# Two attention blocks on one core: output projection of the last chunks taken head by head, and loads issued in order of deadline

## The chip, the cores and the metric

The kernel runs on one core of one Trainium2 chip. The metric is the device time of one execution in microseconds (us). A profile comes from one execution, whose span is about 1.7 us shorter than its device time.

## The reference

Two independent problems, A and B, of the same shape are computed and their results laid side by side. B = 16 batches, 144 queries each, model width 448, 16 heads of width 256, and a cache of 512 keys and values per batch and head, all bf16:

```python
q = (x @ wq).reshape(B, Sq, H, Dh).transpose(0, 2, 1, 3)
scores = einsum("bhqd,bhkd->bhqk", q, k_cache) * (Dh ** -0.5)
p = softmax(scores, axis=-1)
o = einsum("bhqk,bhkd->bhqd", p, v_cache)
return o.transpose(0, 2, 1, 3).reshape(B, Sq, H * Dh) @ wo
```

The caches are nearly all of the data: 67 MB of K and 67 MB of V for each problem.

## The kernel before

The kernel is one software pipeline over 512 units (problem, batch, head). A small scheduler in Python walks through *slots*; in slot i each engine receives one step of several units at different stages. TensorE (PE) gets, in this order: Q projection of unit i+15, every eighth slot the scores of the last 32 query rows of eight units at once (**SB**), scores of the first 112 rows of unit i+5 (**SA**), transposes of the probabilities of unit i+2 (**TA**, and every fourth slot **TB**), probabilities times values of unit i (**PV**), and then some matmuls of the output projection (**OP**). K is loaded with a DMA transpose in groups of eight units (2 MB), V in groups of four (1 MB); three buffers hold each. The SyncE queue (SP) issues all loads strictly in program order, and a load whose buffer is still in use makes SP wait.

The loads were planned by slot:

```python
plan(s_min, t_load_x, 0)
plan(s_min, t_load_wq, 0, 0)                    # ... 0,1 and 0,2
plan(s_min, t_load_k, 0)                        # K group 0
# ... the fourth wq group, V groups 0 and 1
for wg in range(NWG):
    plan(s_min + 1, t_load_wo, 0, wg)           # all of wo, ahead of K group 1
# ...
for SG in range(1, NSG):
    plan(max(s_min, 8 * (SG - NK) + 7 - LS + 1, 8 * SG - 19), t_load_k, SG)   # needed in slot 8*SG-7
for G in range(2, NG):
    plan(max(s_min + 2, 4 * G - 8, 4 * (G - NV) + 3 + 1), t_load_v, G)        # needed in slot 4*G
```

The output is projected in chunks of 128 rows: 32 matmuls that add up in one PSUM bank. A chunk starts only when all heads of its batches are there:

```python
if h == H - 1:                                   # last head of a batch
    # ... for each chunk r that is now complete:
    for p in range(NPC):
        fifo.append((r, p, i + OP_DELAY))
if i >= 0:
    credit += OP_RATE                            # 2.25 matmuls a slot
if i >= NT:
    credit += 4 * OPP
while fifo and fifo[0][2] <= i and credit >= OPP:    # OPP = 2
    credit -= OPP
    # ... take one pair of matmuls; after the last pair evict the bank and store
```

## Time and profile before

| | before |
|---|---|
| time, median of the first 4 runs | 1220.0 us (1219.55 to 1220.79) |
| span of the profile | 1217.8 us |
| PE busy | 1173.1 us, 96% |
| PE waiting for K group 1 | 13.6 us |
| PE waiting for x and wq at the start | 10.5 us |
| after the last PV | 20.0 us |

From the page of before: the span, busy time of each engine with its share of the span, and the shares of the chain of waits that ended last.

```profile
span 1217.8 us, 33870 instructions
PE 1173.1 (96%) x13952; PEld 903.2 (74%) x13952; DVE 770.3 (63%) x2178; ACT 747.9 (61%) x2214; POOL 677.6 (56%) x682
PE 93%; SPq 3%; DMA 2%; DVE 1%; ACT 1%; POOL 0%; issue 0%; ACTq 0%
```

PE is both the busiest engine and the chain. What can be won without touching its work is the time in which it stands still, as far as the trace shows it as idle (e5 finds time that it doesn't show). The wait table of PE in before says where (total us, times, longest):

```profile
PE sb_ps L341 <- DMA kt_sb<-in_A_k_cache_dram: 13.6, 1, 13.6
PE qp_ps L314 <- DMA wq_sb<-in_A_wq_dram: 10.5, 1, 10.5
PE op_ps L538 <- ACT ost_sb L551: 4.4, 4, 1.3
```

SP's timeline in before (start, us of issue, what) shows why K group 1 is late:

```profile
7.83 13.56 SPq L290 DMA_TRANSPOSE kt_sb<-in_A_k_cache_dram  x1
...
22.60 1.14 SPq L299 DMA_DIRECT2D v_sb<-in_A_v_cache_dram  x2
23.79 14.16 SPq L269 DMA_DIRECT2D wo_sb<-in_A_wo_dram  x8
37.99 21.01 SPq L290 DMA_TRANSPOSE kt_sb<-in_A_k_cache_dram  x2
```

Eight wo loads, not needed before slot 17, take 14.16 us of issue ahead of a K that is needed in slot 1. PE's timeline at that place ends each line with the idle time before it and its releaser:

```profile
37.91 0.66 PE L314 MATMUL qp_ps<-xt_sb,wq_sb 128*128 128x144 bf16 x8
52.14 1.90 PE L341 MATMUL sb_ps<-kt_sb,qt_sb 128*32 128x512 bf16 x16 [13.56 <-DMA kt_sb<-in_A_k_cache_dram]
```

And the tail, again PE's timeline: the last two PV, then two chunks of 32 OP matmuls that stand alone:

```profile
1196.68 1.16 PE L503 MATMUL ot_ps<-pt_sb,v_sb 128*128 128x144 bf16 x16
1198.34 6.23 PE L538 MATMUL op_ps<-wo_sb,ring 128*128 128x448 bf16 x32 [0.50 <-ACT ring L518]
1205.27 6.23 PE L538 MATMUL op_ps<-wo_sb,ring 128*128 128x448 bf16 x32 [0.69 <-ACT ost_sb L551]
```

### The profile page before, as it was taken

To read this page: it belongs to the slowest core of one execution; us is meant where nothing else is said; L and a number is where in the kernel's file an instruction comes from. 1 tells how busy PE (TensorE), PEld (TensorE's weight loads), DVE (VectorE), ACT (ScalarE), POOL (GpSimd) and SP (SyncE) were. 2 spreads that over 40 slices of the span, in tenths; PEclk is the share of its full clock that TensorE was granted. 3 is DMA by queue.
4 is the path that set the end of the run, shared out by engine and by line. 5 is a ranking of instruction groups with operands and counts; after the bars stand their busy time and mean duration, and the time that the engine had idled before them with its cause. 6 is when DMAs were issued, how large, how long until landed. Compare 5 with 4: busy or idle time off the path is not lost.

```text
span 1217.8 us, 33870 instructions
## 1 busy us (share of the span) xinstructions
PE 1173.1 (96%) x13952; PEld 903.2 (74%) x13952; DVE 770.3 (63%) x2178; ACT 747.9 (61%) x2214; POOL 677.6 (56%) x682
## 2 busy tenths in 40 slices
PE   4499999999999999999999999999999999999997
PEld 3377777777777777777777777777777777777774
DVE  2377666666666666666666666666666666666661
ACT  1366666666666665666666665666666666666662
POOL 0356556555655655655655655655655665565562
PEclk9799999999999999999999999999999999999999
DMA  9999999999999999999999999999999999999940
GB/s 256 283 242 268 258 262 246 247 234 238 231 255 245 242 241 237 241 244 244 285 268 264 308 276 260 234 244 259 233 239 237 256 236 233 228 243 237 243 153 12
DMA packets 627033, 294.15 MB, mean 242 GB/s; under 512 B 548416, under 2 KB 556608, under 8 KB 626880
## 3 DMA queue, kind: packets, MB, share of 16 engines
q1 hardware_dynamic: 625152, 287.85, 102.9%
q0 software_dynamic: 1728, 4.13, 1.4%
q8 instruction: 111, 1.82, 0.6%
q14 instruction: 42, 0.34, 0.1%
HBM read 148.90 MB, written 4.13 MB: 126 GB/s over the span
## 4 chain that ended last, share of the span: by engine, by line
PE 93%; SPq 3%; DMA 2%; DVE 1%; ACT 1%; POOL 0%; issue 0%; ACTq 0%
PE ot_ps L503 20%; PE qp_ps L314 20%; PE sa_ps L417 19%; PE op_ps L538 18%; PE sa_ps L470 8%; PE sb_ps L341 5%; PE sb_ps L393 2%; DMA kt_sb<-in_A_k_cache_dram 1%; SPq L269 1%; SPq L290 1%; DMA v_sb<-in_B_v_cache_dram 1%; DVE stat L428 1%; SPq L261 0%; ACT pa_sb L439 0%; ACT ost_sb L551 0%
## 5 line engine op out<-in xcount | busy, mean ns | idle before, releaser
L457 POOL TENSOR_TENSOR pa_sb<-pa_sb,stat 112x512 bf16<-112x512 bf16 x512 | 532.0, 1039 | 490.9 <-DVE stat L449 490.6
L439 ACT ACTIVATE pa_sb<-sa_ps,stat 112x512 bf16<-112x512 f32 x512 | 352.0, 688 | 424.2 <-DVE stat L428 423.8
L428 DVE TENSOR_REDUCE stat<-sa_ps 112x1 f32<-112x512 f32 x512 | 353.8, 691 | 301.5 <-PE sa_ps L417 299.0
L314 PEld LDWEIGHTS qp_ps<-xt_sb,wq_sb 128*128 128x128 bf16 x4096 | 292.4, 99 | 99.7 <-issue 11.3
L314 PE MATMUL qp_ps<-xt_sb,wq_sb 128*128 128x144 bf16 x4096 | 344.6, 228 | 16.3 <-DMA wq_sb<-in_A_wq_dram 10.5
L503 PE MATMUL ot_ps<-pt_sb,v_sb 128*128 128x144 bf16 x4096 | 340.8, 226 | 0.8 <-DMA v_sb<-in_B_v_cache_dram 0.8
L417 PE MATMUL sa_ps<-kt_sb,qt_sb 128*112 128x512 bf16 x1024 | 310.1, 384 | 1.2 <-DVE pt_sb L480 0.8
L538 PE MATMUL op_ps<-wo_sb,ring 128*128 128x448 bf16 x1152 | 291.6, 352 | 4.9 <-ACT ost_sb L551 4.4
L503 PEld LDWEIGHTS ot_ps<-pt_sb,v_sb 128*128 128x128 bf16 x4096 | 268.9, 98 | 1.1 <-DMA v_sb<-in_B_v_cache_dram 0.9
L470 PEld LDWEIGHTS sa_ps<-ident,pa_sb 112*128 112x128 bf16 x2048 | 163.1, 113 | 102.7 <-ACT pa_sb L439 17.3
L518 ACT ACTIVATE ring<-ot_ps 128x288 bf16<-128x288 f32 (+8 forms) x512 | 190.0, 371 | 2.5 <-PE ot_ps L503 2.4
L480 DVE COPY pt_sb<-sa_ps 128x448 bf16<-128x448 bf16 x512 | 190.2, 371 | 1.7 <-PE sa_ps L470 1.7
L325 DVE TENSOR_SCALAR qt_sb<-qp_ps 128x288 bf16<-128x288 f32 x256 | 117.0, 457 | 116.0 <-PE qp_ps L314 116.0
L470 PE MATMUL sa_ps<-ident,pa_sb 112*128 112x112 bf16 x2048 | 186.0, 213 | 0.5 <-ACT pa_sb L439 0.5
L381 POOL TENSOR_TENSOR pb_sb<-pb_sb,stat 128x512 bf16<-128x512 bf16 x128 | 132.9, 1039 | 27.2 <-DVE stat L373 27.2
L417 PEld LDWEIGHTS sa_ps<-kt_sb,qt_sb 128*112 128x112 bf16 x1024 | 97.2, 130 | 36.6 <-issue 27.2
L329 ACT ACTIVATE qt_sb<-qp_ps 128x288 bf16<-128x288 f32 x256 | 105.9, 414 | 21.9 <-PE qp_ps L314 21.9
L538 PEld LDWEIGHTS op_ps<-wo_sb,ring 128*128 128x128 bf16 x1152 | 96.6, 98 | 29.7 <-ACT ost_sb L551 6.2
L439 ACT ACTIVATION_READ_ACCUMULATOR pa_sb<-sa_ps,stat 112x1 f32 x512 | 99.2, 194 | 0.0
L353 DVE TENSOR_REDUCE stat<-sb_ps 128x1 f32<-128x512 f32 x128 | 86.9, 679 | 4.6 <-PE sb_ps L341 4.6
L363 ACT ACTIVATE pb_sb<-sb_ps,stat 128x512 bf16<-128x512 f32 x128 | 88.4, 691 | 2.1 <-DVE stat L353 2.1
L341 PE MATMUL sb_ps<-kt_sb,qt_sb 128*32 128x512 bf16 x1024 | 68.6, 389 | 14.7 <-DMA kt_sb<-in_A_k_cache_dram 13.6
(20 smaller groups left out, 366.5 us busy)
## 6 DMA issues: line engine op xcount, KB each, us to landing
v_sb<-in_A_v_cache_dram SPq DMA_DIRECT2D x64, 1024.0 KB, 6.2
v_sb<-in_B_v_cache_dram SPq DMA_DIRECT2D x64, 1024.0 KB, 6.2
out_dram<-ost_sb POOLq DMA_DIRECT2D x36, 112.0 KB, 6.7
wo_sb<-in_A_wo_dram SPq DMA_DIRECT2D x8, 448.0 KB, 8.5
wo_sb<-in_B_wo_dram SPq DMA_DIRECT2D x8, 448.0 KB, 7.2
wq_sb<-in_A_wq_dram SPq DMA_DIRECT2D x4, 768.0 KB, 6.4
wq_sb<-in_B_wq_dram SPq DMA_DIRECT2D x4, 768.0 KB, 7.6
wq_sb<-in_A_wq_dram SPq DMA_DIRECT2D x4, 128.0 KB, 7.0
```

Source lines behind the costliest of these rows:

```text
L314: ins = t.matmul(qp_ps[:, dc * SQ:(dc + 1) * SQ], lhsT=wq_sb[:, kc, c0:c0 + 128], rhs=xt_sb[:, xsl, kc, xo:xo + SQ], start=(kc == 0), stop ...
L341: ins = t.matmul(sb_ps[jj // 4][32 * j:32 * j + 32, :], lhsT=qt_sb[:, U % NQT, dc, QA:SQ], rhs=kt_sb[:, ksl, dc, jj * SK:(jj + 1) * SK], s ...
L381: return g.tensor_tensor(pb_sb[:, psl, :], pb_sb[:, psl, :], stat[:, RINVB + sl:RINVB + sl + 1].to_broadcast([128, SK]), op=ALU.mult)
L417: ins = t.matmul(sa_ps[bank][0:QA, :], lhsT=qt_sb[:, U % NQT, dc, 0:QA], rhs=kt_sb[:, ksl, dc, ko:ko + SK], start=(dc == 0), stop=(dc == 1))
L428: return v.tensor_reduce(stat[0:QA, NEG + sl:NEG + sl + 1], sa_ps[bank][0:QA, :], axis=AX.X, op=ALU.max, negate=True)
L439: return a.activation(pa_sb[0:QA, psl, :], sa_ps[bank][0:QA, :], AF.Exp, bias=stat[0:QA, NEG + sl:NEG + sl + 1], scale=1.0, accum_out=stat ...
L457: return g.tensor_tensor(pa_sb[0:QA, psl, :], pa_sb[0:QA, psl, :], stat[0:QA, RINV + sl:RINV + sl + 1].to_broadcast([QA, SK]), op=ALU.mult)
L470: ins = t.transpose(pta_ps[bank][:, c * 128:c * 128 + QA], src[:, c, :], ident[0:QA, 0:QA])
L480: return v.tensor_copy(pt_sb[:, sl, :, 0:QA], pta_ps[bank][:, 0:512].rearrange("p (c q) -> p c q", c=4)[:, :, 0:QA])
L503: ins = t.matmul(ot_ps[ob][:, dc * SQ:(dc + 1) * SQ], lhsT=v_sb[:, vsl, j, c * DH + dc * 128:c * DH + (dc + 1) * 128], rhs=pt_sb[:, sl, c, ...
L518: ins = a.activation(ring[:, 2 * h:2 * h + 2, c0:c0 + n1], src[:, :, 0:n1], AF.Copy)
L538: ins = t.matmul(op_ps[0:m, 0:D], lhsT=ring[:, c, col0:col0 + m], rhs=wo_sb[:, c, :], start=(c == 0), stop=(c == NWO - 1))
```

## The change

Its intent: (1) the last two chunks are projected head by head during the last 16 units, one in the OP bank and one in the Q projection's bank, which is free by then; (2) every load gets a deadline (the slot of its first use), and loads are issued in the order of deadlines, so that wo no longer stands ahead of K. With it came smaller things: after an eviction of the OP bank no OP for the rest of that slot and in the next one (`op_hold`, the "two-slot hold" below); OP is taken with a credit of 1 instead of 2; more credit in the last 30 slots; the Q projection accumulates with the two halves interleaved; the first SB goes ahead of a Q; there is a third output buffer, and the chunk in the Q bank is evicted by VectorE (DVE).

Cut to its core:

```diff
-            if i >= NT:
+            if i >= u_tail0 - 14:
+                credit += 4.0
+            if i >= NT:
                 credit += 4 * OPP
-            while fifo and fifo[0][2] <= i and credit >= OPP:
-                credit -= OPP
-                r, p, _s = fifo.pop(0)
-                t_op_piece(r, p)
+            for bank in ("op", "qp"):
+                while fifo[bank] and fifo[bank][0][2] <= i and credit >= 1 and (bank == "qp" or i >= op_hold):
+                    r, cs = pop_items(bank, i, OPP)
+                    credit -= len(cs)
+                    t_op_piece(r, cs, bank)
   ... (evict and store after the last piece)
+                        if bank == "op":
+                            op_hold = i + 2
   ... (per head, in the last 16 units)
+                if u >= u_tail0:
+                    for r in tail_chunks:
+                        for dc in range(2):
+                            fifo[tail_bank[r]].append((r, 2 * h + dc, i + 1))
   ... (loads)
+        for wg in range(NWG):
+            plan(s_min, H - 4 + 2 * wg, 10 ** 6, t_load_wo, 0, wg)
+        for SG in range(NSG):
+            dl = 8 * SG - LSB
+            lo = 8 * (SG - NK) + 7 - LS + 1 if SG >= NK else s_min
+            plan(lo, dl, 12, t_load_k, SG)
+        for G in range(NG):
+            dl = 4 * G
+            lo = 4 * (G - NV) + 3 + 1 if G >= NV else s_min
+            plan(lo, dl, 8, t_load_v, G)
+        dma_plan.sort(key=lambda t: t[:2])       # by deadline
+        for dl, sq, lo, lead, fn, args in dma_plan:
+            _prev = max(_prev, lo, dl - lead)    # a running maximum: nothing overtakes
```

Interleaving the two halves of Q in one bank needs care with the start flag, which only the first matmul now carries. The Trainium skill (PSUM — Partial Sum Buffer, "The four PSUM rules") says that this flag clears the written marks of the whole 2 KiB bank, so that the second half's first matmul overwrites, too.

A V that must wait for its buffer now holds back a K with a later deadline, although that K's own lead is longer.

More of the change, by code (lines that the diff above doesn't have):

```diff
@@ L164, in bass_concat_heads__mha_block_cached__gqa_block_cached__near_ridge_kernel @@
     XB = 4 if Bn % 4 == 0 else (2 if Bn % 2 == 0 else 1)
-    NQT, NPA, NPB, NPT, NST, NSTB, NOST = 12, 5, 2, 8, 4, 2, 2
+    NQT, NPA, NPB, NPT, NST, NSTB, NOST = 12, 5, 2, 8, 4, 2, 3
     RS = 4
@@ L310, in e @@
                 ins = None
-                for dc in range(2):
-                    for kc in range(4):
+                for kc in range(4):
+                    for dc in range(2):
                         c0 = h * DH + dc * 128
                         ins = t.matmul(qp_ps[:, dc * SQ:(dc + 1) * SQ], lhsT=wq_sb[:, kc, c0:c0 + 128],
-                                       rhs=xt_sb[:, xsl, kc, xo:xo + SQ], start=(kc == 0), stop=(kc == 3))
+                                       rhs=xt_sb[:, xsl, kc, xo:xo + SQ], start=(kc == 0 and dc == 0),
+                                       stop=(kc == 3), skip_group_check=True)
                 return ins
-            S.add(PE, e, reads=[(("wq", hg), pr), ("wqz", 0), (("xt", xsl), XG)], writes=[("qp", U)],
+            S.add(PE, e, reads=[(("wq", hg), pr), ("wqz", 0), (("xt", xsl), XG)], writes=[("qp", ("q", U))],
                   banks=["qp"], name="Q%d" % U)
@@ L325, in e @@
                     return v.tensor_scalar(qt_sb[:, sl, :, :], src, 1.0 / 16.0, None, op0=ALU.mult)
-                S.add(DVE, e, reads=[("qp", U)], writes=[(("qt", sl), U)], banks=["qp"], name="eq%d" % U)
+                S.add(DVE, e, reads=[("qp", ("q", U))], writes=[(("qt", sl), U)], banks=["qp"], name="eq%d" % U)
             else:
@@ L329, in e @@
                     return a.activation(qt_sb[:, sl, :, :], src, AF.Copy, scale=1.0 / 16.0)
-                S.add(ACT, e, reads=[("qp", U)], writes=[(("qt", sl), U)], banks=["qp"], name="eq%d" % U)
+                S.add(ACT, e, reads=[("qp", ("q", U))], writes=[(("qt", sl), U)], banks=["qp"], name="eq%d" % U)
         def t_sb(SG):
@@ L521, in e @@
                 return ins
-            S.add(ACT, e, reads=[(("otp", ob), U)], writes=[(("ring", r % RS), r) for r in chunks_of_batch(pr, b)],
+            S.add(ACT, e, reads=[(("otp", ob), U)], writes=[(("ring", r % RS, h), r) for r in chunks_of_batch(pr, b)],
                   banks=["ot%d" % ob], name="eot%d" % U)
@@ L529, in chunk_rows, with t_op_piece @@
             return pr, row0, m
-        def t_op_piece(r, p):
+        def t_op_piece(r, cs, bank):
             pr, row0, m = chunk_rows(r)
             col0 = (r % RS) * 128
+            acc = op_ps if bank == "op" else qp_ps
+            key = "opp" if bank == "op" else "qp"
+            first, last = op_first[r], op_last[r]
             def e(t):
                 ins = None
-                for c in range(p * OPP, (p + 1) * OPP):
-                    ins = t.matmul(op_ps[0:m, 0:D], lhsT=ring[:, c, col0:col0 + m], rhs=wo_sb[:, c, :],
-                                   start=(c == 0), stop=(c == NWO - 1))
+                for c in cs:
+                    ins = t.matmul(acc[0:m, 0:D], lhsT=ring[:, c, col0:col0 + m], rhs=wo_sb[:, c, :],
+                                   start=(c == first), stop=(c == last))
@@ L540, in e @@
                 return ins
             nb = len([b for b in range(Bn) if r in chunks_of_batch(pr, b)])
-            assert len(S.res[("ring", r % RS)].writers) == nb * H, (r, nb, len(S.res[("ring", r % RS)].writers))
-            S.add(PE, e, reads=[(("ring", r % RS), r), (("wo", (p * OPP) // WOG), pr)], writes=[("opp", r)],
-                  banks=["op"], name="OP%d.%d" % (r, p))
-        def t_evac_op(r):
+            rd = []
+            for hh in sorted(set(c // 2 for c in cs)):
+                assert len(S.res[("ring", r % RS, hh)].writers) == nb, (r, hh, nb)
+                rd.append((("ring", r % RS, hh), r))
@@ L547, in t_evac_op, with e @@
+            S.add(PE, e, reads=rd + [(("wo", wg), pr) for wg in sorted(set(c // WOG for c in cs))],
+                  writes=[(key, ("o", r))], banks=[bank], name="OP%d.%d" % (r, cs[0]))
+        def t_evac_op(r, bank, eng):
             pr, row0, m = chunk_rows(r)
             sl = r % NOST
-            def e(a):
-                return a.activation(ost_sb[0:m, sl, :], op_ps[0:m, 0:D], AF.Copy)
-            S.add(ACT, e, reads=[("opp", r)], writes=[(("ost", sl), r)], banks=["op"], name="eop%d" % r)
+            acc = op_ps if bank == "op" else qp_ps
+            key = "opp" if bank == "op" else "qp"
+            if eng == ACT:
+                def e(a):
+                    return a.activation(ost_sb[0:m, sl, :], acc[0:m, 0:D], AF.Copy)
+            else:
+                def e(v):
+                    return v.tensor_copy(ost_sb[0:m, sl, :], acc[0:m, 0:D])
+            S.add(eng, e, reads=[(key, ("o", r))], writes=[(("ost", sl), r)], banks=[bank], name="eop%d" % r)
@@ L566, in bass_concat_heads__mha_block_cached__gqa_block_cached__near_ridge_kernel, with plan @@
         t_ident()
-        dma_plan = {}
-        def plan(slot, fn, *args):
-            dma_plan.setdefault(slot, []).append((fn, args))
+        dma_plan = []
+        def plan(lo, deadline, lead, fn, *args):
+            dma_plan.append((deadline, len(dma_plan), lo, lead, fn, args))
         s_min = -LQ - 24
-        plan(s_min, t_load_x, 0)
-        plan(s_min, t_load_wq, 0, 0)
-        if HG > 1:
-            plan(s_min, t_load_wq, 0, 1)
-        if HG > 2:
-            plan(s_min, t_load_wq, 0, 2)
@@ L579, in bass_concat_heads__mha_block_cached__gqa_block_cached__near_ridge_kernel @@
-        plan(s_min, t_load_k, 0)
-        for hg in range(3, HG):
-            plan(s_min, t_load_wq, 0, hg)
-        plan(s_min, t_load_v, 0)
-        if NG > 1:
-            plan(s_min, t_load_v, 1)
-        for wg in range(NWG):
-            plan(s_min + 1, t_load_wo, 0, wg)
-        x_last_reader = {}
         for XG in range(NXGT):
             pr, j = divmod(XG, Bn // XB)
-            u_last = pr * NU + (j + 1) * XB * H - 1
-            x_last_reader[XG] = u_last - LQ
-        for XG in range(1, NXGT):
-            pr, j = divmod(XG, Bn // XB)
@@ L594, in bass_concat_heads__mha_block_cached__gqa_block_cached__near_ridge_kernel @@
             u_first = pr * NU + j * XB * H
-            lo = x_last_reader[XG - NXG] + 1 if XG >= NXG else s_min
-            plan(max(s_min, lo, u_first - LQ - 40), t_load_x, XG)
-        for SG in range(1, NSG):
-            plan(max(s_min, 8 * (SG - NK) + 7 - LS + 1, 8 * SG - 19), t_load_k, SG)
-        for G in range(2, NG):
-            plan(max(s_min + 2, 4 * G - 8, 4 * (G - NV) + 3 + 1), t_load_v, G)
-        for pr in range(1, NP):
-            for hg in range(HG):
-                plan(pr * NU - H + 4 * hg + 3 - LQ + 1, t_load_wq, pr, hg)
@@ L605, in bass_concat_heads__mha_block_cached__gqa_block_cached__near_ridge_kernel @@
-        fifo = []
+            dl = u_first - LQ
+            if XG >= NXG:
+                pr0, j0 = divmod(XG - NXG, Bn // XB)
+                lo = pr0 * NU + (j0 + 1) * XB * H - 1 - LQ + 1
+            else:
+                lo = s_min
+            plan(lo, dl, 40, t_load_x, XG)
+        for pr in range(NP):
+            for hg in range(HG):
+                dl = pr * NU + 4 * hg - LQ
+                lo = pr * NU - H + 4 * hg + 3 - LQ + 1 if pr > 0 else s_min
+                plan(lo, dl, 10 ** 6, t_load_wq, pr, hg)
@@ new lines, in bass_concat_heads__mha_block_cached__gqa_block_cached__near_ridge_kernel @@
+        for wg in range(NWG):
[9 more added lines that the diff above has]
+        dma_plan.sort(key=lambda t: t[:2])
+        _prev = s_min
+        _tmp = []
@@ new lines, in bass_concat_heads__mha_block_cached__gqa_block_cached__near_ridge_kernel @@
+        for dl, sq, lo, lead, fn, args in dma_plan:
+            _prev = max(_prev, lo, dl - lead)
+            _tmp.append((_prev, dl, sq, fn, args))
+        dma_plan = _tmp
+        u_tail0 = NT - H
+        pr_l, b_l, _h = unit(NT - 1)
+        tail_chunks = []
+        g_end_l = pr_l * RP + (b_l + 1) * SQ
+        for r in range((pr_l * RP + b_l * SQ) // 128, (g_end_l - 1) // 128 + 1):
+            tail_chunks.append(r)
+        tail_chunks = tail_chunks[-2:]
+        tail_bank = {}
+        if tail_chunks:
+            tail_bank[tail_chunks[-1]] = "qp"
+            if len(tail_chunks) > 1:
+                tail_bank[tail_chunks[0]] = "op"
@@ L606, in bass_concat_heads__mha_block_cached__gqa_block_cached__near_ridge_kernel, with queue_chunk, pop_items @@
+        op_first, op_last = {}, {}
+        fifo = {"op": [], "qp": []}
         stores = []
         credit = 0.0
+        op_hold = -10 ** 9
         OP_RATE = float(NCH * NWO) / NU
         last_chunk_of = {pr: (pr + 1) * NCH - 1 for pr in range(NP)}
+        def queue_chunk(r, ready):
+            op_first[r], op_last[r] = 0, NWO - 1
+            for c in range(NWO):
+                fifo["op"].append((r, c, ready))
+        def pop_items(bank, i, n):
+            q = fifo[bank]
+            r = q[0][0]
+            cs = []
+            while q and len(cs) < n and q[0][0] == r and q[0][2] <= i:
+                cs.append(q.pop(0)[1])
+            return r, cs
@@ L610, in bass_concat_heads__mha_block_cached__gqa_block_cached__near_ridge_kernel @@
         i = s_min
         while True:
-            for fn, args in dma_plan.pop(i, []):
+            while dma_plan and dma_plan[0][0] <= i:
+                _sl, _dl, _sq, fn, args = dma_plan.pop(0)
                 fn(*args)
@@ L629, in bass_concat_heads__mha_block_cached__gqa_block_cached__near_ridge_kernel @@
                 t_store(stores.pop(0)[0])
+            if do_sb and sgi == 0:
+                t_sb(sgi)
             u = i + LQ
@@ L633, in bass_concat_heads__mha_block_cached__gqa_block_cached__near_ridge_kernel @@
                 t_evac_q(u)
-            if do_sb:
+            if do_sb and sgi > 0:
                 t_sb(sgi)
@@ L663, in bass_concat_heads__mha_block_cached__gqa_block_cached__near_ridge_kernel @@
                 pr, b, h = unit(u)
+                if u >= u_tail0:
+                    for r in tail_chunks:
+                        if h == 0:
+                            op_first[r], op_last[r] = 0, NWO - 1
+                        for dc in range(2):
+                            fifo[tail_bank[r]].append((r, 2 * h + dc, i + 1))
                 if h == H - 1:
@@ L668, in bass_concat_heads__mha_block_cached__gqa_block_cached__near_ridge_kernel @@
                         r_end = min((r + 1) * 128, pr * RP + Bn * SQ)
-                        if g_end >= r_end:
-                            for p in range(NPC):
-                                fifo.append((r, p, i + OP_DELAY))
+                        if g_end >= r_end and r not in tail_bank:
+                            queue_chunk(r, i + OP_DELAY)
             if i >= 0:
                 credit += OP_RATE
+            if i >= u_tail0 - 14:
+                credit += 4.0
             if i >= NT:
                 credit += 4 * OPP
-            while fifo and fifo[0][2] <= i and credit >= OPP:
-                credit -= OPP
-                r, p, _s = fifo.pop(0)
-                t_op_piece(r, p)
-                pr = r // NCH
-                if r == last_chunk_of[pr] and pr + 1 < NP and (p * OPP) % WOG == WOG - OPP:
-                    t_load_wo(pr + 1, (p * OPP) // WOG)
-                if p == NPC - 1:
-                    t_evac_op(r)
-                    stores.append((r, i + 2))
-            if not fifo:
+            for bank in ("op", "qp"):
[3 more added lines that the diff above has]
+                    t_op_piece(r, cs, bank)
+                    pr = r // NCH
+                    if r == last_chunk_of[pr] and pr + 1 < NP:
+                        for c in cs:
+                            if c % WOG == WOG - 1:
+                                t_load_wo(pr + 1, c // WOG)
+                    if cs[-1] == op_last[r]:
+                        t_evac_op(r, bank, ACT if bank == "op" else DVE)
+                        stores.append((r, i + (2 if i < NT else 0)))
+                        if bank == "op":
+                            op_hold = i + 2
+            if not fifo["op"] and not fifo["qp"]:
                 credit = min(credit, 2.0 * OPP)
             i += 1
-            if i >= NT and not fifo and not dma_plan and not stores:
+            if i >= NT and not fifo["op"] and not fifo["qp"] and not dma_plan and not stores:
                 break
```

## The prediction

> **What bounds it now.** TensorE. The page gives PE 1173.1 of 1217.8 us (96%), the chain of waits is 93% PE. PE's idle 45 us: 10.5 us at the start for x and wq (wait table); 13.6 us at 38.5-52.1 us for the second K group; half-microsecond waits for evictions during the first Q projections; 4.4 us before output projections (OP) for the eviction of op_ps; and the end. DMA is close behind: about 242 GB/s throughout, SP issuing without a pause until about 145 us.
>
> **Loads at the start.** SP's timeline shows K0's issue ending at 21.4, then wq3, V0, V1, then eight wo loads (14.2 us of issue), and only then K1, issued at 38.0, landed at 52.1. The change issues K1 right after V0 and spreads wo behind it. K1 then lands at about 39, so the stall shrinks to 0-2 us. The stall also chilled PE: the windows view shows clock 0.50 at 52-56 us, and SB took 1.90 us against 1.05. The Trainium skill (TensorE: Matmul & The Clock Gate, "The HAM clock gate") says that an idle window of about 3.4 us halves the clock; the trace agrees. Together 13.6 + 2 us.
>
> Not all of it stays. The queue is saturated: a period of one K and two V costs about 16.4 us, PE consumes one in 15.8-19.6 us, and the wo loads are only postponed. I estimate K2..K7 landing 0-3 us late each; net gain by the eighth group about 6 us (3-12).
>
> **Loads later.** Sorting by deadline with a running maximum of slots puts K behind a V that waits for its buffer: K is issued about 9 slots (20 us, sometimes 18.5) before its use, before 12. Median issue-to-landing is 15.7 us, so it usually holds, but x loads (4.2 + 1.3 us of issue) now sit directly ahead of a K, and at the change of problem x and wq0 do. Where before paid only 0.8 us (for V, near 700 us), I expect 3-8 us of K waits at 590-720 us, and 0-2 us at each other x load. Loss about 6 us.
>
> **Tail.** Before, after the last PV (1197.8), 32 + 32 OP matmuls run alone (2 x 6.24 us). The change spreads them per head over the last 16 units, in two banks. But PE is nearly full there: a slot without Q lasts 1.78 us through the loop SA, max, reciprocal, copy, with about 0.2 us free next to one OP pair. So 12.5 us move and are not removed. Removed are only PE gaps: 0.5 + 0.7 + 0.7 + about 1 us. Final eviction, store and landing (6 us) stay. Gain 2-3 us.
>
> **Other.** The two-slot hold after an op_ps eviction saves up to 3 us in the middle. Q's loop order and SB0 ahead of Q8: within 1 us.
>
> Sum: -6 + 6 - 2.5 - 3 = about -6 us: **1214 us**, range **1203 to 1226**. Chances: faster by over 2% 0.04, within 2% 0.93, slower 0.03.
>
> **What would show it.** Right: no 13.6 us wait for K1, clock near 1.0 from 30 us on; smaller PE waits for kt_sb (total 5-20 us) in the first 150 us, near 590-720 us and at x loads; last PV 6-9 us before the end instead of 20; PE busy about 1170. Wrong: K waits nowhere later (then about 1200), or in most groups (then over 1225).
>
> **What would make it wrong.** Transfers landing faster or slower than the medians in this order; OP bursts (22 in one slot) starving the DVE loop; a stall over 3.4 us cooling PE again.

## The result, and the profile after

| | before | changed |
|---|---|---|
| time, median | 1219.81 us (13 runs) | 1215.43 us (9 runs, 1213.76 to 1216.72) |
| ratio, 95% interval | | 0.9963 (0.9954 to 0.9973) |
| span of the profile | 1217.8 us | 1209.9 us |
| PE busy | 1173.1 us | 1175.1 us |
| PE waits for K | 13.6 us, 1 time | 9.1 us, 7 times |
| from the end of the last PV to the end | 20.0 us | 8.1 us |

A ratio is the mean time of one kernel's runs over the mean of the other's in the same rounds, so it is not quite the ratio of the medians quoted. The changed kernel is 0.4% faster, and this is clear of noise. The outputs are right. Its profiled execution took 1211.66 us, less than any of the nine timed ones, so the profile is used for places, and the rounds for the size of the whole.

From the page after:

```profile
span 1209.9 us, 33868 instructions
PE 1175.1 (97%) x13952; PEld 902.0 (75%) x13952; DVE 769.7 (64%) x2179; ACT 752.8 (62%) x2213; POOL 678.7 (56%) x682
PE 90%; DMA 6%; DVE 1%; SPq 1%; ACT 0%; issue 0%; POOL 0%; ACTq 0%
```

The chain now runs 6% of the span through DMA, where it was 2%. PE's wait table after:

```profile
PE qp_ps L314 <- DMA wq_sb<-in_A_wq_dram: 10.6, 1, 10.6
PE sb_ps L342 <- DMA kt_sb<-in_A_k_cache_dram: 6.3, 5, 1.8
...
PE sb_ps L342 <- DMA kt_sb<-in_B_k_cache_dram: 2.8, 2, 2.3
```

One long wait for K became seven short ones; the wait for the OP eviction is gone. SP's timeline after, at the start:

```profile
22.86 0.59 SPq L299 DMA_DIRECT2D v_sb<-in_A_v_cache_dram  x1
23.49 13.32 SPq L290 DMA_TRANSPOSE kt_sb<-in_A_k_cache_dram  x1
36.86 1.13 SPq L299 DMA_DIRECT2D v_sb<-in_A_v_cache_dram  x2
38.03 14.45 SPq L290 DMA_TRANSPOSE kt_sb<-in_A_k_cache_dram  x1
52.53 0.58 SPq L269 DMA_DIRECT2D wo_sb<-in_A_wo_dram  x1
```

K group 1 is issued at 23.49 us, not 37.99, and wo begins at 52.53. PE's timeline there:

```profile
38.84 0.66 PE L314 MATMUL qp_ps<-xt_sb,wq_sb 128*128 128x144 bf16 x8
39.54 1.05 PE L342 MATMUL sb_ps<-kt_sb,qt_sb 128*32 128x512 bf16 x16
```

SB starts at 39.54 us instead of 52.14 and takes 1.05 us instead of 1.90. The tail after (PE's timeline):

```profile
1201.20 0.66 PE L504 MATMUL ot_ps<-pt_sb,v_sb 128*128 128x144 bf16 x8
1201.70 0.54 PE L542 MATMUL op_ps<-wo_sb,ring 128*128 128x448 bf16 x2
1202.08 0.54 PE L542 MATMUL qp_ps<-wo_sb,ring 128*128 128x448 bf16 x2
1202.46 0.54 PE L542 MATMUL op_ps<-wo_sb,ring 128*128 128x448 bf16 x2
1202.84 0.54 PE L542 MATMUL qp_ps<-wo_sb,ring 128*128 128x448 bf16 x2
```

Only eight OP matmuls follow the last PV. But the last PV itself ends at 1201.86 us, *later* than before (1197.84).

**The ledger.** Both kernels run 64 SBs, one for each K group, so the start of each SB is a milestone that can be compared between traces. The table cuts the profile of each kernel at the SBs of groups 8, 31, 36 and 61 (177, 592, 683 and 1138 us in before) and gives how much each stretch is longer (+) or shorter (−) than in before. The rows below the second belong to the experiments. An *empty slot* is one in which no OP matmul is issued.

| us against before, by stretch | start to 8 | 8 to 31 | 31 to 36 | 36 to 61 | 61 to end | span |
|---|---|---|---|---|---|---|
| changed, first profile | −8.1 | +0.7 | +3.2 | −1.8 | −1.8 | −7.9 |
| changed, second profile (r_after) | −7.9 | +0.7 | +3.4 | −1.8 | −1.7 | −7.3 |
| loads only (e1) | −6.9 | +0.2 | +3.8 | −1.0 | 0.0 | −3.8 |
| all but loads (e2) | +0.4 | +0.7 | +0.3 | −1.8 | −1.7 | −2.1 |
| changed, no hold (e3) | −4.8 | +1.3 | +4.7 | −0.6 | −0.5 | +0.2 |
| changed, no added empty slots (e5) | −5.0 | −0.9 | +4.6 | −3.0 | −1.9 | −6.2 |
| changed, no wo traffic (e6) | −12.7 | +0.7 | +3.8 | −1.8 | −1.7 | −11.7 |
| changed, loads in slots of before, wo late (e4) | −7.0 | +0.7 | +0.3 | −1.3 | −1.7 | −9.0 |
| changed, K ahead again after the start (e10) | −8.2 | +0.7 | +0.3 | −1.5 | −1.7 | −10.4 |
| put together (e9) | −9.2 | −2.3 | −0.6 | −3.4 | −3.1 | −18.7 |

### The profile page after: what moved, and what is told of

It reads as the page before. It is cut to its first block, busy times and chain, and to the rows that moved or that the text cites. A ratio compares the mean times of both kernels' runs of the same rounds, so it can differ in the third digit from the quotient of the medians.

```text
span 1209.9 us, 33868 instructions
## 1 busy us (share of the span) xinstructions
PE 1175.1 (97%) x13952; PEld 902.0 (75%) x13952; DVE 769.7 (64%) x2179; ACT 752.8 (62%) x2213; POOL 678.7 (56%) x682
## 4 chain that ended last, share of the span: by engine, by line
PE 90%; DMA 6%; DVE 1%; SPq 1%; ACT 0%; issue 0%; POOL 0%; ACTq 0%
PE qp_ps L314 20%; PE ot_ps L504 19%; PE sa_ps L418 18%; PE op_ps L542 17%; PE sa_ps L471 8%; PE sb_ps L342 5%; DMA kt_sb<-in_A_k_cache_dram 4%; PE sb_ps L394 2%; DMA kt_sb<-in_B_k_cache_dram 2%; DVE stat L429 1%; DMA wq_sb<-in_A_wq_dram 1%; PE qp_ps L542 0%; SPq L280 0%; SPq L281 0%; DVE qt_sb L326 0%
## 5 line engine op out<-in xcount | busy, mean ns | idle before, releaser
L314 PE MATMUL qp_ps<-xt_sb,wq_sb 128*128 128x144 bf16 x4096 | 344.3, 228 | 16.4 <-DMA wq_sb<-in_A_wq_dram 10.6
L542 PE MATMUL op_ps<-wo_sb,ring 128*128 128x448 bf16 x1120 | 278.8, 352 | 0.0
L450 DVE RECIPROCAL stat<-stat 112x1 f32<-112x1 f32 x512 | 78.1, 152 | 0.5 <-ACT pa_sb L440 0.5
```

What stands on the lines that cost most here:

```text
L314: ins = t.matmul(qp_ps[:, dc * SQ:(dc + 1) * SQ], lhsT=wq_sb[:, kc, c0:c0 + 128], rhs=xt_sb[:, xsl, kc, xo:xo + SQ], start=(kc == 0 and dc ...
L542: ins = t.matmul(acc[0:m, 0:D], lhsT=ring[:, c, col0:col0 + m], rhs=wo_sb[:, c, :], start=(c == first), stop=(c == last))
```

## The experiments

Eleven kernels ran in three sets (e1 to e4; r_after, e5, e6 and e9; e7, e8 and e10). Those of one set ran on the same chip and share its runs of before. Ratios are to before of the same set.

### e1: the loads alone

Before, with only the plan of loads replaced by the deadline plan of the change.

> Before with the deadline order of loads alone; tail, hold and Q order as before. Theory: the whole start gain and the whole later loss are in the loads: the 13.6 us wait for K1 and about 2 us of cold clock go, 8 to 13 us of small K waits come, in the first 150 us and near 600-625 us. Expected 3 to 6 us under before (ratio 0.995 to 0.9975), with the 3 waits of 1.3 us for the op_ps eviction still there. Rival (gain is in the tail): within 1 us of before.

Measured: 1216.43 us, ratio 0.9982 (0.9968 to 0.9996), so about 2 us; in its profile 3.8 us of span. K waits 10.2 us (7 waits for A, 1 for B), eviction waits 4.4 us as before. The theory of where holds: 6.9 us won at the start, 3.8 lost between groups 31 and 36, nothing in the tail. By the rounds the gain fell just short of the range. They alone don't exclude the rival, whose 1 us lies inside the interval (0.5 to 3.9 us); the profile, with 6.9 us at the start and 0.0 in the tail, speaks against it.

### e2: everything but the loads

The changed kernel with the load plan of before.

> The changed kernel with the loads in the order of before: tail per head, hold and Q order alone. Theory: tail gains about 3 us; the hold saves 3 x 1.3 us but costs 0.2 us at each chunk end. Expected 1 to 3.5 us under before (ratio 0.997 to 0.999), K1 wait of 13.6 us still there. Rival (the 12.5 us of exposed output projection are really removed): 10 us or more under before.

Measured: 1217.68 us, ratio 0.9992 (0.9978 to 1.0006), about 1 us and not clear of noise; 2.1 us of span in the profile. The K wait is back at 13.1 us. The tail (61 to end) gave 1.7 us, not 12.5: the rival, that the exposed projection is removed, falls. The wait table has no OP eviction, yet that did not show as a gain of 3.8 us before the tail. Between groups 1 and 61 this kernel won only 0.5 us, although three waits of 1.3 us and a V wait of 0.8 us were gone. About 4 us (3.8 + 0.8 − 0.5) must have been paid somewhere; e5 finds it.

### e3: without the hold

```diff
-                            op_hold = i + 2
+                            op_hold = i
```

> The changed kernel without the two-slot hold after an op_ps eviction. Prediction on record: the hold saves up to 3 us, so this is 3 us slower than the changed kernel. Theory now, from the traces: a slot without output projection makes the next SA and TA wait, 0.2 us per chunk end, some 5 us in all, against 3.8 us of eviction waits saved; so this is 0 to 2 us faster than the changed kernel (about 1214), and waits for the eviction of about 4 us come back.

Measured: 1219.74 us, ratio 1.000 (0.9984 to 1.0016). The expectation failed: the prediction's sign was right and the new theory's wrong. Four eviction waits of 5.1 us in total came back, as both said. But not all of the distance is the hold's. This profile is 8.1 us longer than the first of the changed kernel, and 3.3 us of that lie in "start to 8" and 1.5 in "31 to 36", where PE waits for loads whose order is the same in both; each of the two stretches also has 3.4 us at half clock here and none in the changed kernel (see the cold clock below). In the two stretches without load waits the sum is +0.7 us here and −1.1 in the changed kernel, and the tail gained 1.3 us less; so the hold as such is worth 2 to 3 us. What it buys and what it costs are separated by e5.

### e5: no added empty slots

```diff
-                while fifo[bank] and ... and credit >= 1 and (bank == "qp" or i >= op_hold):
+                while fifo[bank] and ... and credit >= (OPP if bank == "op" and i < u_tail0 - 14 else 1) and (bank == "qp" or i >= op_hold):
...
-                            op_hold = i + 2
+                            op_hold = i + 1
```

> The changed kernel, but an output projection is taken only with credit for a whole pair, as in before, and the hold lasts only for the rest of its own slot. Counted in the program, slots without an output projection before the last 30 fall from 75 to 45, the number of before. Theory: each such slot costs 0.15 us of PE (1.78 us loop against 1.63 us of work), so 30 x 0.15 = 4.5 us faster than the changed kernel, with no wait for the eviction. Rival (credit and hold do not matter, the drift has another cause): equal to the changed kernel.

Measured: 1210.47 us, ratio 0.9928 (0.9916 to 0.994), against 0.9955 for the changed kernel in the same set: 3.3 us faster where 4.5 had been expected, with no eviction wait. In the profile the stretches 8 to 31 and 36 to 61 are 2.8 us shorter than in the changed kernel, while its K waits were longer that time (12.6 us), as "start to 8" and "31 to 36" show. The rival falls. Why an empty slot costs, PE's timeline of the changed kernel shows, from a slot with OP into two without:

```profile
209.28 0.92 PE L542 MATMUL op_ps<-wo_sb,ring 128*128 128x448 bf16 x4
210.03 0.66 PE L314 MATMUL qp_ps<-xt_sb,wq_sb 128*128 128x144 bf16 x8
210.53 0.59 PE L418 MATMUL sa_ps<-kt_sb,qt_sb 128*112 128x512 bf16 x2
210.96 0.36 PE L471 MATMUL sa_ps<-ident,pa_sb 112*128 112x112 bf16 x4
211.16 0.67 PE L504 MATMUL ot_ps<-pt_sb,v_sb 128*128 128x144 bf16 x8
211.66 0.66 PE L314 MATMUL qp_ps<-xt_sb,wq_sb 128*128 128x144 bf16 x8
212.27 0.64 PE L418 MATMUL sa_ps<-kt_sb,qt_sb 128*112 128x512 bf16 x2
...
215.37 0.66 PE L314 MATMUL qp_ps<-xt_sb,wq_sb 128*128 128x144 bf16 x8
215.97 0.64 PE L418 MATMUL sa_ps<-kt_sb,qt_sb 128*112 128x512 bf16 x2
...
217.15 0.66 PE L314 MATMUL qp_ps<-xt_sb,wq_sb 128*128 128x144 bf16 x8
```

The first empty slot lasts 1.63 us (210.03 to 211.66), which is PE's work. After it SA starts 0.6 us after Q and no longer 0.5, and the slots settle at 1.78 us (215.37 to 217.15). SA writes the bank that DVE has just copied the transposed probabilities out of, and that copy (211.84 to 212.21 us in DVE's timeline, SA at 212.27) comes after a maximum of 0.69 us on the same engine. With an OP pair in the slot this loop is hidden; without one, PE waits 0.15 us. The cost falls on the slot *after* an empty one, whether that is empty or not: measured against 2.01 us for a slot with one OP pair and 0.19 us for each matmul more or less (slots with SB or TB against their own), the 57 slots of this profile that follow an empty one in the stretches 8 to 31 and 36 to 61 are longer by 0.13 us on average, 7.2 us in all. The waits do not show as idle in the busy times, because PE's modelled ends overlap: PE is "97% busy" throughout. The Trainium skill (Perfetto Trace Analysis, "Identifying the Most-Contended Engine") says that matmul busy time is not a good measure of how close a kernel is to roofline. Busy time *rose* by 2.0 us in the changed kernel, which was faster, with the same 13952 matmuls. The page's reason, that pipelined instructions look smaller in the trace, is not what is seen here, where busy time hides waits.

### e6: the bytes of wo taken away

```diff
+            if pr == 0:
+                # on POOL, before the first slot: memset(wo_sb[...], 0.0) instead of the load
```

> Wrong result on purpose: the output weights of the first problem are zeroed on the chip in the first microseconds and not loaded; order of all else as in the changed kernel. Theory: the K waits of the first 150 us are the wo bytes (3.67 MB, 14 us of issue in before) postponed and not removed, on a saturated queue; without them the K waits there fall from 4 to 8 us to under 2 us, and the eighth group starts 5 to 7 us earlier than in the changed kernel. Rival (K waits come from K standing behind a V): they stay at 4 us or more.

Measured: 1208.56 us, ratio 0.9915 (0.9901 to 0.9929); the result is wrong. Its wait table has one K wait for A, of 1.3 us and for group 0, in place of five or six, and none later in the first 150 us. Group 8 starts 4.8 us earlier than in the changed kernel's second profile; 5 to 7 had been expected. So the short waits at the start are caused by the 3.67 MB of wo on a queue that is full, not by K standing behind a V, which it still does here. The B waits (3.4 us near group 32) stayed.

### e4: slots of before, only wo late

The changed kernel with all loads planned as in before, except that V group 1 and wo are planned behind K group 1 and x loads come 24 slots ahead instead of 40.

```diff
-            plan(s_min, t_load_v, 1)
-        for wg in range(NWG):
-            plan(s_min + 1, t_load_wo, 0, wg)
+            plan(-4, t_load_v, 1)
+        for wg in range(NWG):
+            plan((5, 5, 5, 9, 9, 13, 13, 14)[wg], t_load_wo, 0, wg)
```

> The changed kernel with the slots of before for all loads (K 12 slots ahead of use and not behind a V), only V1 and the wo loads moved behind K1 and x loads at lead 24. Theory: the start is limited by what the queue moves, so its small K waits (4 to 7 us) stay; the K waits near 600-625 us go, as K gets its 3 slots back. Expected 2 to 4 us faster than the changed kernel, about 1212. Rival (small K waits are a matter of order): no K wait at all, about 1206.

Measured: 1209.77 us, ratio 0.9925 (0.9913 to 0.9938), so about 9 us under before, twice the gain of the change. PE's wait table of this run has two lines of load waits after the first Q, this one, and one wait of 0.5 us for V of B at 712 us:

```profile
PE ot_ps L504 <- DMA v_sb<-in_A_v_cache_dram: 5.8, 3, 3.2
```

There is no K wait at all, as the rival had it and not the theory, and still 5.8 us are lost in the first 150 us: with K ahead, it is V that comes late. The order only chooses who waits, the shortage at the start stays. The loss at 31 to 36 is gone (+0.3 instead of +3.2 to 3.4).

### e10: K ahead again, after the start only

```diff
-            _prev = max(_prev, lo, dl - lead)
-            _tmp.append((_prev, dl, sq, fn, args))
-        dma_plan = _tmp
+            if dl <= 41:
+                _prev = max(_prev, lo, dl - lead)
+                _tmp.append((_prev, dl, sq, fn, args))
+            else:
+                _tmp.append((max(_prev, lo, dl - lead), dl, sq, fn, args))
+        dma_plan = sorted(_tmp, key=lambda t: t[:3])
```

The lead of x is 16 slots instead of 40, so that it doesn't fall into the start.

> The changed kernel with deadline order for the first six K groups only, then K 12 slots ahead of its use as in before and x 16 slots ahead of their first Q. Theory: the 3 us of K waits at 590-630 us, where x, wq and a V stand ahead of K, go, and with them the jitter there; the K waits of the first 150 us stay. Expected 2.5 to 5 us under the changed kernel, ratio to before 0.991 to 0.994. Rival (the queue itself is short at that place, whatever the order): K or V waits of 3 us stay.

Measured: 1210.33 us, ratio 0.9928 (0.9913 to 0.9943). The wait table has no load wait at all after 155 us; 6.2 us of K and 0.8 of V remain before. The loss near group 32 was therefore made by the order. The lead of x, changed as well, is not the reason: e2 has the old slots with a lead of 40, and loses only 0.3 us there. SP's timeline of the changed kernel shows it: x, wq and a V in front of the K that is needed at 584 us.

```profile
558.33 5.69 SPq L299 DMA_DIRECT2D v_sb<-in_A_v_cache_dram  x2
564.07 3.08 SPq L280 DMA_TRANSPOSE xt_sb<-in_B_x_dram  x1
567.19 2.14 SPq L281 DMA_TRANSPOSE xt_sb<-in_B_x_dram  x1
569.38 0.58 SPq L259 DMA_DIRECT2D wq_sb<-in_B_wq_dram  x1
570.00 1.74 SPq L261 DMA_DIRECT2D wq_sb<-in_B_wq_dram  x1
571.78 8.69 SPq L290 DMA_TRANSPOSE kt_sb<-in_A_k_cache_dram  x1
```

In before the same K was issued at 562.87 us. The two K groups behind it, issued at 584.93 and 604.42, then came late; before had issued them at 580.90 and 602.05.

### e7: what the long stall cost beyond its length

Before, with 60 matmuls on data at hand, into the OP bank (unused then), in front of the second SB.

> Before, with 60 idle-time matmuls of ident and wq into the unused op_ps bank ahead of the second SB, inside the 13.6 us stall; they must end before K1 lands. Theory: the stall costs more than its length, because PE's clock drops; kept warm, SB1 takes 1.05 instead of 1.90 us and the step from SB1 to SB2 falls from 17.95 to 15.8 us. Expected 1.5 to 2.5 us under before (ratio about 0.998) with 60 matmuls more. Rival (no cost beyond the wait): equal to before or slower.

Measured: 1218.95 us, ratio 0.9996 (0.9982 to 1.001). The whole time can't be told from before. The place can: in the windows view, the rows of 52 to 56 us (us, busy time and count of PE, PEld, DVE, ACT, POOL, then PE clock, DMA share, GB/s) are, first in before, then in e7:

```profile
52.00:56.00 4.00, 3.86 (x29) 2.08 (x30) 0.90 (x3) 0.17 (x1) 0.06 (x1) 0.50 1.27 270
```

```profile
52.00:56.00 4.00, 2.45 (x35) 1.67 (x36) 0.79 (x3) 0.07 (x1) 0.00 (x0) 1.00 1.11 235
```

The clock is 1.00 instead of 0.50, and SB takes 1.05 us:

```profile
39.16 11.51 PE L638 MATMUL op_ps<-wq_sb,ident 128*128 128x448 bf16 x60
53.55 1.05 PE L341 MATMUL sb_ps<-kt_sb,qt_sb 128*32 128x512 bf16 x16 [2.88 <-DMA kt_sb<-in_A_k_cache_dram]
```

From this SB to the next it is 15.84 us, against 17.95 in before: 2.1 us. In this profile K landed 1.4 us later than in before's, so only 0.7 us of it was left at group 2; whether the matmuls had a part in that lateness, no run tells.

### e8: less work in the tail

```diff
+                        if r == tail_chunks[-1] and h not in (0, H - 1):
+                            continue
```

> Wrong result on purpose: the changed kernel with the last chunk's projection cut to 2 of 16 heads, 28 of its 32 matmuls (28 x 0.19 = 5.3 us of PE) left out of the last 16 slots. Theory: PE is full there, so the projection was moved and not hidden; the time falls by 3.5 to 4.5 us against the changed kernel (5.3 us less about 1.3 us where the slots fall to the 1.78 us loop). Rival (projection hides in PE's gaps): within 1 us of the changed kernel.

Measured: 1212.78 us, ratio 0.9936 (0.992 to 0.9952), wrong result. The changed kernel had 0.9963 and 0.9955 in other sets, which puts the difference at 2.3 to 3.3 us, below the range. In its profile, K waits were 11.1 us, more than in either profile of the changed kernel. The stretch that was altered is cleaner: from the SB of group 63 to the end it is 38.0 us, against 41.1 in both profiles of the changed kernel, so 3.1 us came off. Most of what was cut was therefore on PE's path; where the slots fell to two OP matmuls the loop took over (one SA there waits 0.21 us for DVE), as expected, by somewhat more than expected. The rival, within 1 us, falls.

### r_after: the changed kernel again

> The changed kernel once more, unaltered, as a yardstick on the chip of this call and for a second profile. Expected 0.996 to 0.997 of before; K waits of 8 to 13 us in all, not of the same length at the same places as in the first profile, since they depend on when transfers land; everything else the same to 0.1 us.

Measured: 1214.73 us (1212.25 to 1214.97), ratio 0.9955 (0.9943 to 0.9966). K waits 9.9 us. The rows of the ledger agree within 0.3 us. Over all profiles with the deadline order and wo loaded (both of the changed kernel, e1, e3, e5, e8) the K waits were 9.1 to 12.6 us and the gain at group 8 was 4.8 to 8.1 us.

### e9: the findings put together

Deadline order for the start only (as in e10), credit for whole pairs and a hold for the rest of the slot only (as in e5), and two more changes: credit is capped at 4.5, which ends the bursts of ten OP matmuls and the empty slots after them, and the extra credit starts 14 slots later.

```diff
-            if i >= u_tail0 - 14:
+            if i >= u_tail0:
                 credit += 4.0
+            if i < u_tail0:
+                credit = min(credit, 4.5)
```

> A version put together from the findings: deadline order for the first six K groups only, then the slots of before (K 12 ahead of use), x loads 16 slots ahead; output projections of at most 4.5 credits at a time and never twice around an eviction in a slot (16 slots without one, before 45, changed 75); extra credit only in the last 16 slots. Expected: 4 to 6 us of K waits at the start, none later, no drift; about 1203 (ratio 0.985 to 0.989).

Measured: 1200.2 us (1198.17 to 1200.86), ratio 0.9839 (0.9827 to 0.9852), correct, and faster than both kernels, by more than expected. Its page and wait table:

```profile
span 1199.1 us, 33869 instructions
PE 1167.7 (97%) x13952; PEld 906.3 (76%) x13952; DVE 770.7 (64%) x2179; ACT 755.3 (63%) x2213; POOL 678.4 (57%) x682
```

```profile
PE sb_ps L342 <- DMA kt_sb<-in_A_k_cache_dram: 5.9, 4, 2.2
...
PE ot_ps L504 <- DMA v_sb<-in_B_v_cache_dram: 0.6, 1, 0.6
```

Counted in the instruction order between slot 17 and the last 16 units, empty slots number 46 in before, 84 in the changed kernel, 63 in e3, 54 in e5 and 16 here. By the 0.13 us that e5's section measures for an empty slot (0.13 us in this profile, too, over 11 slots), 68 fewer than in the changed kernel are worth about 9 us, an estimate from those numbers. The ledger shows somewhat less: of the 10.8 us between the profiles of the changed kernel and e9, 4.6 lie in the stretches 8 to 31 and 36 to 61, where 46 of the 68 are (and where e9 waited 0.6 us for a V), 1.3 in the tail, 1.1 at the start, and 3.8 in 31 to 36, the loads. No run splits e9 further. The ratios are 14 us apart, more than the profiles, which show the changed kernel's fastest execution and e9's slowest.

## Why the prediction was right or wrong

The time was right, 1214 predicted against 1215.43 us measured, and so was the mechanism of most of its parts. Two terms were mis-sized in opposite directions, and one cost was missing; that the sum came so close is in part luck.

- **The start: right.** "net gain by the eighth group about 6 us (3-12)". Six profiles gave 4.8 to 8.1. That the rest of 13.6 + 2 us is lost to wo, which is "only postponed", is shown by e6 and e4: without the bytes 12.7 us stay, and with another order V waits instead of K.
- **The cold clock: right.** The step from the second SB to the third costs 2.1 us more when the clock has dropped (e7). The Trainium skill (TensorE: Matmul & The Clock Gate, "The HAM clock gate") has the clock halve after an idle window of about 3.4 us; in the trace it is 0.50 at 52 to 56 us after 13.6 us idle, and 1.00 when the idle time was filled. In the changed kernel's two profiles the short K waits, at most 2.3 us, brought no cold stretch. But waits under 3.4 us can: in the profiles of e1, e3, e5, e8 and e9 K waits of 1.8 to 3.0 us were followed by 3.41 us at half clock, once or twice in each. In e1 it was a wait of 1.83 us (a line of PE's timeline, then a row of the windows view in the columns of e7):

```profile
113.01 1.05 PE L341 MATMUL sb_ps<-kt_sb,qt_sb 128*32 128x512 bf16 x16 [1.83 <-DMA kt_sb<-in_A_k_cache_dram]
114.33:117.75 3.42, 3.42 (x19) 2.12 (x18) 1.65 (x4) 1.75 (x5) 1.04 (x1) 0.50 1.05 381
```

The length of the wait alone does not decide it: 1.83 us cooled PE here, and the 2.88 us left in e7 did not. What fits all the profiles is how busy PE was in the 3.41 us before, on a grid of 3.41 us on which all recorded clock steps lie (stretches of full or half clock last 1, 4, 5, 14, 20 and more whole times 3.41 us). From the first recorded step to 1190 us, every window at most 0.41 busy was followed by half clock, every window over 0.47, outside a stretch already cold, by full clock; of four between them one, with 0.46, was followed by half clock. This was read from the traces afterwards, no run tests it, and the ends of matmuls are modelled. One such stretch costs up to 1.7 us (half of 3.41, an estimate); in e1 the stretch 31 to 36 lost 3.8 us with only 2.2 us of K wait in it.
- **Loads later: right in kind and place, too large in size.** "Loss about 6 us", of which "3-8 us of K waits at 590-720 us". The stretch between groups 31 and 36 lost 3.2 to 3.4 us in the changed kernel, and e10 shows that the order made it. The waits of "0-2 us at each other x load" did not come: beyond 155 us no x load other than the one at the change of problem had a K wait behind it in either profile of the changed kernel. In the first 155 us K group 7, behind an x load, waited 0.3 us; and e8's profile has one such wait of 0.6 us, at group 39.
- **The tail: right in kind, a little too large.** "12.5 us move and are not removed", "Gain 2-3 us". The stretch from group 61 to the end gained 1.7 to 1.8 us, with the loads as before (e2) as well as with the new ones, and cutting 28 matmuls there shortens it by 3.1 us (e8). So the gain was a little under the range. The last PV ended 8.1 us before the end, where 6 to 9 were predicted.
- **"Other": the step that failed.** "The two-slot hold after an op_ps eviction saves up to 3 us in the middle." The waits it removes were 3.8 us in the middle, as read from the trace. Taken alone the hold did what was said: without it the two stretches free of load waits are 1.8 us longer and the tail 1.3 us (e3). But the term left out what the hold and the lower credit limit, which the prediction doesn't mention, do to the slots around: 30 more empty slots before the last 30 units (45 before, 75 changed; 54 in e3, so that 21 come with the hold and 9 with the credit limit), each of which costs 0.13 to 0.15 us at DVE's copy, about 4 us in all by e2's ledger. Together these rules were worth about nothing (−0.5 us between groups 1 and 61 in e2), and e5, which keeps the removed waits and drops the added empty slots, is 3.3 us faster than the changed kernel. The prediction had the 1.78 us loop in hand, for the tail, and did not look for it in the middle. Q's loop order and the place of the first SB were not tested alone.

So the sum came out right because a loss overestimated by some 3 us and a gain overestimated by about 3 us cancelled each other. That is luck, and it holds for the sum of the terms; the first profile, 7.9 us under before, gained 2 us more at the start than predicted, and the rounds, 4.4 us under before, less than the sum.

What stays open: how much of the spread of the changed kernel's executions (1211.66 to 1216.72 us) has which cause. The K waits of the six profiles with the deadline order and wo loaded differ by 3.5 us, and cold stretches of up to 1.7 us each come on top, none in the changed kernel's two profiles and one or two in others. The recorded clock fits that in part: in r_after's set the run of 1212.25 us has 0.999 and the four others, up to 1214.97 us, 0.995 to 0.997 (one cold stretch lowers the mean by 0.0014), but in the first set the order is not so clean. No timed run beside the profiled one has a trace.

## What to carry to other kernels

Moving work off an exposed tail gains only the idle time of the engine that has to do it meanwhile; if that engine is full there, the exposed 12.5 us shrink to less than 2. Where the queue is saturated, move what isn't needed soon behind what is, but don't let an item that waits for its buffer hold back another whose buffer is free: K, freed early, lost its lead to a V, and e4, which left K its lead, moved only wo and one V behind it and loaded x a little later, gained twice as much as the full order by deadline. And when an engine is "97% busy", compare the start-to-start times of a repeated step: the cost of an empty slot (1.78 against 1.63 us) stood in no wait table.

## What the Trainium skill lacked or had wrong

- Perfetto Trace Analysis, "Identifying the Most-Contended Engine": it says that matmul busy time misleads, and offers MFU (the matmul work over the window's peak) and LDWEIGHTS busy share instead. Here the work is the same in all kernels, so that MFU only restates the time, and the LDWEIGHTS share moved little (74% before, 75% changed, 76% in e9) while the time fell by 1.6%; what found the gain was the length of one slot, 1.78 against 1.63 us. The page names start-to-start spacing for GpSimd instructions only; it could name it for a repeated step on TensorE.
- TensorE: Matmul & The Clock Gate, "The HAM clock gate": the idle window of about 3.4 us that it gives for the half clock is no safe limit for a single wait. Here K waits of 1.8 to 3.0 us were followed by 3.41 us at 0.50 in five profiles, and others of up to 2.9 us (e7) were not.
- DMA: Bandwidth & Descriptors, "Latency and other measured facts": it gives 261 GB/s for DMA transposes with a non-contiguous middle dimension. In before, between 97 and 130 us, one transposed K group and two plain V groups (4.19 MB) took 16.4 to 16.7 us from issue to issue, 251 to 256 GB/s; half of these bytes are plain, so this doesn't test the page's figure. What decided here, and what the table of that section doesn't have, is that the issue of one such 2 MB transpose held SP for 8.7 to 16.7 us (changed kernel), and every load behind it waited that long.
- None of the pages has the cost of a lead that is just long enough: with K issued 9 slots (about 20 us) ahead, and 15.7 us from issue to landing in before's median, K waits after the first 155 us were 2.2 to 4.2 us in the seven profiles with that order throughout; with 12 slots after the start (e4, e9, e10) there were none.
